# Banded attention and a gated two-layer network on one core: one front moved ahead, units re-dealt to two batches, loads spread anew

## The chip, the core and the metric

The kernel runs on one core of one Trainium2 chip. The metric is the device time of one execution in microseconds, lower is better; the time shown is the median of three runs. The core has five engines that run side by side, each through its own list of instructions in order: PE (TensorE: matmuls and transposes), DVE (VectorE), ACT (ScalarE), POOL (GpSimd) and SP (SyncE, which here only issues DMAs). POOL computes and also issues the loads from memory; an instruction of its list that waits holds up the loads behind it.

## The reference

Attention over a window of 64 keys, for 8 batches of 8 heads, 576 positions and 64 columns a head; then, on the 4608 x 512 result, two matrix products with a gate between them.

```python
scores = scale * np.matmul(q, k.transpose(0, 1, 3, 2))
mask = (rel >= 0) & (rel < window)          # window = 64
attn = softmax(np.where(mask, scores, -1e9))
x = np.matmul(attn, v) ...                  # as 4608 x 512
h = x @ w_in                                # 512 x 2048
g = h * np.clip(h + 3.0, 0.0, 6.0) / 6.0
return g @ w_out                            # 2048 x 512
```

## The kernel before

**Attention** goes by pairs of heads: pair t is heads 2g and 2g+1 of batch b, with b, g = divmod(t, 4); there are 32 pairs. For a pair these steps follow each other:

- `load_qk(b, n, first)` (line 115) issues on POOL the loads of k and then of q for n pairs of batch b, from pair `first` on; 144 KB each for one pair. `load_v(b, part=...)` (131) issues the loads of v in up to three pieces, and `shift(b)` (155) makes on SP a copy of v shifted by 32 partitions.
- `turn(t)` (269): 36 transposes on PE, which put keys and queries of the pair across, into two PSUM banks, tk and tq, of the pool `ps_h`. `turned(t, 0)` copies tk to KT on DVE, `turned(t, 1)` copies tq to QT on ACT (both line 283).
- `s_first(t, host)` and `s_rest(t)` (291, 301): 36 small matmuls, the scores. Those of the first window go into spare columns of the tk and tq banks of another pair, the host; the rest into two banks of `ps_t`.
- `weights(t, ...)` (316): on ACT the exponentials, e0 twice (line 319) and e twice (323); on POOL (batch 1: DVE) three products with the masks, P (328) and Pz twice (331). `front(t, host)` (780) is the scores and the weights together.
- `pv(t)` (383): 40 small matmuls, weights by v, into the pool `ps_o`. `pv_out(t)` (409): six DVE instructions, sums, recs, opg twice, opl twice, which divide by the sums. `x_(t)` (435) turns the result across by DMA transposes on SP into `xT`; for batch 1 `x_turned(t)` (453) does it by five transposes on PE and a copy on ACT.

**The network** goes by blocks of 512 rows, nine in all. A block has 16 first units f0 to f15 (`unit` in `first_units`, 469): four matmuls of 128x512 into one bank, then on ACT t (line 499) and on DVE gT (500); the bank is free when gT is done. It has 16 second units (507), four for each of four groups of 128 rows: four matmuls each over gT into a bank acc; the last of four is followed by a copy osb on ACT (529) and a store. Every unit is thus four matmuls.

**PSUM** has eight banks: `ps_o` two (used as one tile of two), `ps_t` three, `ps_h` two, `ps_acc` one. A tile takes a bank of its pool that was given back; a unit's first matmul waits until the last reader of that bank's former tile is done.

**The order** is written by hand (`manual_schedule`): each engine runs its instructions in the order in which the program gives them. `queue_block(kb, kept, lead)` (540) puts a block's units into a deque, `moe`: first some second units left over from the block before, then the first units with the other left-overs between them, then the block's own second units but for the last `kept`. `weave(n)` takes n units off the front and writes them. `group(t, n)` (752) writes, in this order: pv(t), turn(t+2), the scores and weights of t+1, pv_out(t), the copy KT of t+2, x_(t), two units, the copy QT of t+2, and n - 2 units.

**Around the change** (lines 820 to 868). Batches 0 and 1 have their own order. The loop over t = 4 to 7 does pv of batch 1 and issues loads of batch 2 behind dummy copies (`behind`) that hold POOL back until opg is there. Then come pair 8's turn, the last second units of block 0, the first three quarters of f0 to f3 of block 1 (they lack the last pair, 7), x_turned(7), the last quarters, and group 7, with pair 9's turn, pair 8's scores and four units; behind it on POOL the load of pair 11 and two pieces of v of batch 3. From t = 8 on a group takes 4 units in batch 2 and 8 in each later batch; in the loop the loads of the next batch stand behind the group's products on POOL. While attention runs on, from block 1 on, first units take banks of `ps_t` alone (`late[0] == 1`, line 484).

Of the kernel before, what the change touches and what calls it, by code (L numbers as in the profile page):

```python
# [36 lines left out]
def kernel(  # L37
# [10 lines left out]
    B, H, S, _ = q.shape  # L48
    DM, FF = moe_w_in.shape
    NT = B * S  # L50
    NG = H // 2
# [3 lines left out]
    NFC = FF // P  # L55
# [14 lines left out]
    ps_t = ctx.enter_context(tc.tile_pool(name="ps_t", bufs=3, space=PSUM))  # L70
    ps_h = ctx.enter_context(tc.tile_pool(name="ps_h", bufs=2, space=PSUM))
    ps_acc = ctx.enter_context(tc.tile_pool(name="ps_acc", bufs=1, space=PSUM))
# [42 lines left out]
    def load_qk(b, n=NG, first=0):  # L115
        t = staged[b] if first else stage.tile([P, H, RL * D], BF16, name="qk9", tag="qk")
        hs = slice(2 * first, 2 * (first + n))
        for z, src in enumerate((k, q)):
            nc.gpsimd.dma_start(  # L119
                out=t[halves[z], hs], in_=src[b, hs].rearrange("h (p r) d -> p h (r d)", r=RL)  # L120
            )
        return t
# [8 lines left out]
    def load_v(b, whole=False, part=slice(None)):  # L131
        loads = (
            (0, Un[b % 2][:, 0], 2 * P), (2 * P, Un[b % 2][:, 1], 2 * P),
            *(((W, Us[b % 2][:, 0], 2 * P), (W + 2 * P, Us[b % 2][:, 1], 2 * P)) if whole
              else ((4 * P, Us[b % 2][3 * P // 4 : P, 1], W),)),
        )
        for m, to, n in loads[part]:
            nc.gpsimd.dma_start(  # L138
                out=to[:, :, VO : VO + P],
                in_=v[b, :, m : m + n, :].rearrange("h (p r) d -> p h (r d)", r=2),  # L140
            )
# [13 lines left out]
    def shift(b):  # L155

        un, us = Un[b % 2], Us[b % 2]
        nc.sync.dma_start(out=us[0 : P - 32], in_=un[32:P])
        nc.sync.dma_start(out=us[P - 32 : P, 0], in_=un[0:32, 1])
# [109 lines left out]
    def turn(t):  # L269

        b, g = divmod(t, NG)
        hosts[t] = [ps_h.tile([P, 8 * P], BF16, name=name, tag="bk") for name in ("tk", "tq")]
        for r in range(RL):
            for h in range(2):
                for z in range(2):
                    nc.tensor.transpose(  # L276
                        out=hosts[t][z][halves[h], r * W : (r + 1) * W],
                        in_=staged[b][halves[z], 2 * g + h, r * D : (r + 1) * D],
                        identity=ident[halves[z], halves[z]],
                    )  # L280

    def turned(t, z):
        (nc.scalar.copy if z else nc.vector.tensor_copy)(  # L283
            out=(QT[t % 4][:] if z else KT[t % 4][:, W:]).rearrange("q (p r) -> q p r", r=RL),
            in_=hosts[t][z][:, 0:S].rearrange("q (r p) -> q p r", p=W),
        )
# [177 lines left out]

    gTs = {}
    late = [0]
    halfway, units = {}, {}

    def first_units(kb):
        t0 = kb * TB % XR  # L470
        gT = gpool.tile([P, NFC, TB], BF16, name="gT")
        gTs[kb] = gT

        def unit(fc, gs=range(NG), pool=None, to=None, act=True):
            if fc in halfway:
                hT = halfway.pop(fc)
            elif to is not None:
                hT = to
            else:
                if pool is None:  # L480
                    if late[0] == 0:
                        pool = ps_acc if fc == 8 else ps_h if fc in (5, 6, 11, 12) else ps_t
                    else:
                        pool = ps_t if late[0] == 1 or fc % 2 else ps_h
                hT = pool.tile([P, TB], F32, name="hT", tag="bk")[:]
            for g in gs:
                nc.tensor.matmul(  # L487
                    hT, lhsT=win16[:, g, fc * P : (fc + 1) * P], rhs=xT[:, g, t0 : t0 + TB],
                    start=(g == 0), stop=(g == NG - 1),
                )  # L490
            if gs[-1] == NG - 1 and act:
                hidden(fc, hT)
            else:
                halfway[fc] = hT

        def hidden(fc, hT=None):
            hT = halfway.pop(fc) if hT is None else hT
            t1 = t1pool.tile([P, TB], BF16, name="t1")
            nc.scalar.activation(out=t1[:], in_=hT, func=RELU, bias=half_const[:], scale=1.0 / 6.0)  # L499
            nc.vector.scalar_tensor_tensor(  # L500
                out=gT[:, fc, :], in0=t1[:], scalar=1.0, in1=hT, op0=MIN, op1=MULT
            )

        units[kb] = unit, hidden
        return [lambda fc=fc: unit(fc) for fc in range(NFC)]

    def second_units(kb):
        gT = gTs[kb]
# [27 lines left out]
    moe = deque()  # L536
# [3 lines left out]
    def queue_block(kb, kept=2 * NG, lead=2):  # L540

        f = first_units(kb)
        moe.extend(left[:lead])
        del left[:lead]
        n = len(left)
        for i, unit in enumerate(f):
            moe.extend(left[i * n // NFC : (i + 1) * n // NFC])
            moe.append(unit)
        left[:] = second_units(kb)
        n = len(left) - kept  # L550
        moe.extend(left[:n])
        del left[:n]
# [6 lines left out]
    def pair_bank():  # L559
        both = ps_o.tile([P, 2, 512], F32, name="hTo", tag="o")  # L560
        return [both[:, i] for i in range(2)]

    def complete(kb, fcs, pair=()):
        unit, hidden = units[kb]
        for fc in fcs:
            unit(fc, (NG - 1,), act=fc not in pair)
            if fc in pair[1:]:
                for x in pair:
                    hidden(x)
        for _ in fcs:  # L570
            moe.popleft()

    def weave(n):
        for _ in range(min(n, len(moe))):
            moe.popleft()()
# [94 lines left out]
    staged = {0: load_early_qk((1,))}  # L670
# [64 lines left out]
    u = units[0][0]  # L735
# [16 lines left out]
    def group(t, n):  # L752

        if t >= 2 * NG:
            pv(t)
        if t + 2 < T:
            turn(t + 2)
        if t + 1 < T:
            host = t + 2
            if host >= T:  # L760
                hosts[host] = [ps_h.tile([P, 8 * P], BF16, name=name, tag="bk") for name in ("tk", "tq")]
            s = s_first(t + 1, host)
            weights(t + 1, s, s_rest(t + 1))
        if t >= 2 * NG:
            pv_out(t)
        if t + 2 < T:
            turned(t + 2, 0)
        if t >= 2 * NG:
            x_(t)
        weave(2)  # L770
        if t + 2 < T:
            turned(t + 2, 1)
        weave(n - 2)
# [6 lines left out]
    def front(t, host, muls=(nc.gpsimd,) * 3):  # L780
        s = s_first(t, host)
        weights(t, s, s_rest(t), muls)

    def behind(t):

        nc.gpsimd.tensor_copy(out=seen[:], in_=opgs[t][1][0:1, 0, 0:1])
# [3 lines left out]
    n = NG  # L790
# [29 lines left out]
    for t in range(n, n + 4):  # L820
        pv(t, t % 2 == 0)
        pv_out(t)
        if t < n + 3:
            behind(t)
        if t == n:
            load_v(2, part=slice(1, 3))
        elif t < n + 3:
            load_qk(2, 1, t - n)
        if t > n:
            x_turned(t - 1)  # L830
        if t == n + 2:
            shift(2)
        if t < n + 3:
            weave(1)
    turn_two(2 * NG)
    weave(len(moe))
    late[0] = 1
    queue_block(1)
    u, some = units[1][0], range(NG - 1)
    u(0, some, ps_t)  # L840
    u(1, some, ps_t)
    u(2, some, ps_acc)
    x_turned(n + 3)
    u(3, some, to=pair_bank()[0])
    complete(1, range(4))
    f, z = [moe.popleft() for _ in range(NFC - 4)], list(moe)
    moe.clear()
    moe.extend(f[0:3] + z[0:1] + f[3:6] + z[1:2] + f[6:] + [z[2], z[4], z[3]] + z[5:])
    pads(3, nc.gpsimd.memset)
    group(2 * NG - 1, 4)  # L850
    load_qk(2, 1, 3)
    load_v(3, part=slice(0, 2))
    for t in range(2 * NG, T):
        b, g = divmod(t, NG)
        if g == 0 and b > 2:
            queue_block(b - 1, lead=4 if b == 3 else 2)
        group(t, -(-len(moe) // (NG - g)))
        if b + 1 < B:
            if g == 0:
                staged[b + 1] = load_qk(b + 1, NG if b > 2 else 1)  # L860
            elif b == 2:
                load_qk(b + 1, 1, g)
            if b == 2 and g == 0:
                load_v(b + 1, part=slice(2, 3))
            if b > 2 and g == 1:
                load_v(b + 1)
            if g == 1 + (b > 2):
                shift(b + 1)
    late[0] = 2
    queue_last(NTB - 2)  # L870
# [36 lines left out]
```

## Time and profile before

| | us |
|---|---|
| median of 3 runs | 321.55 (321.15 to 323.0) |
| the profiled execution, in all | 320.98 |
| its span, first to last instruction | 319.3 |
| PE busy | 302.0 |
| ACT busy | 184.3 |
| DVE busy | 181.3 |
| POOL busy | 124.3 |
| mean granted TensorE clock | 0.997 |

The span is shorter than the run by 1.7 us, which lie around it. A busy share is an average: what a stage costs is read from the stage. In the stretch that the change touches, the groups start (first matmul of pv) at 67.99 (pair 8), 72.65 (9), 78.33 (10), 83.81 (11), 88.56 (12), 96.80 (13), 104.97 (14), 113.53 (15) and 121.67 us (16). A line of the trace names the engine, the line of the code, the operation, the tile written and the tiles read; "idle before" and the name behind it say what ended a wait.

### The profile page before, as it was taken

The numbers are of one execution on the slowest core, as the hardware profiler recorded it, in microseconds if no ns is written. First come the engines' busy times: TensorE is split into PE (matmuls) and PEld (weight loads), VectorE is DVE, ScalarE is ACT, GpSimd is POOL, SyncE is SP. The second block draws the span as 40 slices with busy tenths as digits, with TensorE's granted clock in tenths as the row PEclk, the third lists the DMA queues.
The fourth block names the chain that finished last, engine by engine and source line by source line (L and its number), as shares of the span: only waits on it lengthen the run. The fifth ranks groups of instructions, "written<-read, shape, count | busy, mean of one in ns | idle before, by whom it ended". The sixth has DMA issues, their size and how long they took to land.

```text
span 319.3 us, 10688 instructions
## 1 busy us (share of the span) xinstructions
PE 302.0 (95%) x4566; PEld 151.8 (48%) x4608; DVE 181.3 (57%) x415; ACT 184.3 (58%) x345; POOL 124.3 (39%) x168
## 2 busy tenths in 40 slices
PE   7889998998999999999999999999999999999992
PEld 3454454544555455555555555555544444444440
DVE  5766657587737754775377537762776156334200
ACT  2738575586757754776477647764773266454410
POOL 8981206289876335543445345633330000000000
PEclk9999999999999999999999999999999999999998
DMA  6999999939999943994299339934021200100021
GB/s 89 161 210 206 207 192 158 201 51 142 168 140 192 98 118 88 166 130 116 88 158 139 107 100 160 138 105 100 4 69 38 84 33 0 69 33 34 36 75 65
DMA packets 57592, 35.67 MB, mean 112 GB/s; under 512 B 39872, under 2 KB 51648, under 8 KB 57536
## 3 DMA queue, kind: packets, MB, share of 16 engines
q0 software_dynamic: 35904, 18.81, 46.0%
q1 hardware_dynamic: 21632, 16.08, 20.4%
q8 instruction: 38, 0.62, 0.8%
q14 instruction: 18, 0.15, 0.1%
HBM read 37.62 MB, written 9.44 MB: 147 GB/s over the span
## 4 chain that ended last, share of the span: by engine, by line
PE 84%; POOL 5%; DMA 3%; ACT 2%; DVE 2%; issue 2%; POOLq 0%; ACTq 0%; DVEq 0%
PE acc L523 36%; PE hT L487 35%; PE o L404 3%; PE s L310 2%; PE acco L523 2%; PE tk L276 2%; DMA V<-in_v_dram 2%; DMA qk<-in_q_dram 2%; POOL qk L108 2%; POOL Pz L331 1%; PE tq L276 1%; ACT t L499 1%; POOL V L138 1%; POOL qk L119 1%; PE hTo L487 1%
## 5 line engine op out<-in xcount | busy, mean ns | idle before, releaser
L500 DVE SCALAR_TENSOR_TENSOR gT<-t,hT 128x512 bf16<-128x512 bf16 x141 | 95.7, 687 | 78.2 <-ACT t L499 77.2
L487 PE MATMUL hT<-xT,win 128*128 128x512 bf16 x550 | 132.1, 379 | 1.8 <-DVE gT L500 0.6
L523 PE MATMUL acc<-wout,gT 128*128 128x512 bf16 x520 | 126.4, 379 | 2.2 <-issue 1.3
L499 ACT ACTIVATE t<-hT,half_const 128x512 bf16<-128x512 f32 x141 | 95.8, 690 | 48.3 <-PE hT L487 46.5
L487 PEld LDWEIGHTS <-win 128*128 128x128 bf16 x576 | 55.5, 98 | 66.6 <-issue 2.0
L523 PEld LDWEIGHTS <-gT 128*128 128x128 bf16 x576 | 54.5, 98 | 63.2
L331 POOL TENSOR_TENSOR Pz<-e,band 128x512 bf16<-128x512 bf16 x48 | 54.3, 1149 | 0.0
L328 POOL TENSOR_TENSOR P<-e,first 64x256 bf16<-64x256 bf16 x24 | 16.0, 666 | 88.7 <-ACT e L319 88.7
L529 ACT COPY osb<-acc 128x512 f32<-128x512 f32 x34 | 19.9, 586 | 43.1 <-PE acc L523 40.2
L323 ACT ACTIVATE e<-s 128x512 bf16<-128x512 f32 x56 | 30.1, 590 | 0.2 <-issue 0.2
L283 DVE COPY KT<-tk 128x576 bf16<-128x576 bf16 x28 | 21.0, 750 | 5.3 <-ACT e L319 4.5
L138 POOL DMA_DIRECT2D V<-in_v_dram x22 | 17.9, 818 | 8.8 <-DMA wout<-in_moe_w_out_dram 4.6
L428 DVE TENSOR_TENSOR opl<-o,recs 128x256 bf16<-128x256 f32 x52 | 19.7, 420 | 0.5
L283 ACT COPY QT<-tq 128x576 bf16<-128x576 bf16 x28 | 17.8, 637 | 1.5 <-PE tq L276 1.5
L413 DVE TENSOR_REDUCE sums<-o 128x10 f32<-128x20 f32 x26 | 4.6, 176 | 23.6 <-PE o L404 23.6
L404 PEld LDWEIGHTS <-Pz 64*64 64x64 bf16 x1008 | 11.5, 108 | 12.9 <-issue 9.8
L319 ACT ACTIVATE e<-tk 64x128 bf16<-64x128 f32 x28 | 7.6, 271 | 15.1 <-PE tq L296 15.1
L276 PE MATMUL tq<-ident,qk 64*64 64x64 bf16 x504 | 13.9, 195 | 0.6 <-DMA qk<-in_q_dram 0.6
L310 PE MATMUL s<-QT,KT 64*64 64x64 bf16 x896 | 14.1, 195 | 0.4 <-DVE gT L500 0.4
L404 PE MATMUL o<-V,Pz 64*64 64x65 bf16 x936 | 13.6, 195 | 0.8 <-POOL Pz L331 0.8
L276 PE MATMUL tk<-ident,qk 64*64 64x64 bf16 x504 | 14.0, 195 | 0.0
L276 PEld LDWEIGHTS <-qk 64*64 64x64 bf16 x1008 | 11.6, 106 | 2.9 <-issue 2.1
(102 smaller groups left out, 195.9 us busy)
## 6 DMA issues: line engine op xcount, KB each, us to landing
out_dram<-osb SPq DMA_DIRECT2D x36, 256.0 KB, 2.2
V<-in_v_dram POOLq DMA_DIRECT2D x16, 256.0 KB, 5.5
V<-V SPq DMA_DIRECT2D x6, 432.0 KB, 4.3
qk<-in_k_dram POOLq DMA_DIRECT2D x4, 576.0 KB, 7.0
qk<-in_q_dram POOLq DMA_DIRECT2D x4, 576.0 KB, 9.5
wout<-in_moe_w_out_dram POOLq DMA_DIRECT2D x2, 1024.0 KB, 17.3
qk<-in_q_dram POOLq DMA_DIRECT2D x12, 144.0 KB, 4.0
qk<-in_k_dram POOLq DMA_DIRECT2D x12, 144.0 KB, 4.0
```

The lines of the kernel that those rows point to most:

```text
L138: nc.gpsimd.dma_start(out=to[:, :, VO : VO + P], in_=v[b, :, m : m + n, :].rearrange("h (p r) d -> p h (r d)", r=2),)
L276: nc.tensor.transpose(out=hosts[t][z][halves[h], r * W : (r + 1) * W], in_=staged[b][halves[z], 2 * g + h, r * D : (r + 1) * D], identity= ...
L283: (nc.scalar.copy if z else nc.vector.tensor_copy)(out=(QT[t % 4][:] if z else KT[t % 4][:, W:]).rearrange("q (p r) -> q p r", r=RL), in_= ...
L310: nc.tensor.matmul(ss[h][halves[i], c, m, r], lhsT=keys(t, h, W * (w - 1), r), rhs=QT[t % 4][halves[h], w * W : (w + 1) * W], start=True, ...
L323: nc.scalar.activation(out=e[:].rearrange("p c m r w -> p (c m r w)"), in_=ss[h][:].rearrange("p c m r w -> p (c m r w)"), func=EXP, scale ...
L331: muls[h].tensor_tensor(out=Pw[t % 4][:, h].rearrange("p c m r w -> p (c m) (r w)"), in0=e[:].rearrange("p c m r w -> p (c m) (r w)"), in1 ...
L404: nc.tensor.matmul(o[i][halves[c], c0 : c0 + D + 1], lhsT=p, rhs=vt[:, hh, v0 : v0 + D + 1], start=(r == 0), stop=(r == 1), skip_group_che ...
L487: nc.tensor.matmul(hT, lhsT=win16[:, g, fc * P : (fc + 1) * P], rhs=xT[:, g, t0 : t0 + TB], start=(g == 0), stop=(g == NG - 1),)
L499: nc.scalar.activation(out=t1[:], in_=hT, func=RELU, bias=half_const[:], scale=1.0 / 6.0)
L500: nc.vector.scalar_tensor_tensor(out=gT[:, fc, :], in0=t1[:], scalar=1.0, in1=hT, op0=MIN, op1=MULT)
L523: nc.tensor.matmul(acc, lhsT=gT[:, fc, ts * P : (ts + 1) * P], rhs=wout16[:, fc, :], start=(fc == 0), stop=(fc == NFC - 1),)
L529: nc.scalar.copy(out=osb[:], in_=acc)
```

## The change

- **Front of pair 8.** Of block 1 only f0 and f1 have their first three quarters ahead of pair 7's result, f0 in the `ps_o` banks. Then come pair 9's turn and pair 8's scores and weights; then the last quarters of f0 and f1, f2 to f6 whole, and the first second unit. Group 7 is gone as a group; its parts are written out. Eight units of block 1 are written ahead of group 8, as before.
- **Loads.** Pair 10's load leaves the loop over t = 4 to 7. Pairs 10 and 11 are loaded together, 288 KB each for k and q, behind pair 8's products on POOL, followed by one piece of v of batch 3 in place of two. In batch 2, groups 8, 9 and 10 issue the loads of pairs 12, 13, and 14 with 15; v's second piece follows group 8, the third group 9. The shift of batch 3 stays behind group 9. From batch 3 on the loads of the next batch are as before.
- **Units.** Block 1 keeps four second units for later instead of eight. Batch 2 takes five units a group, batch 3 seven, in the order written in `arrange`. There a number from 0 up is a first unit; -1 is the first of the second units in the deque, -2 the second, and so on. Its first units take banks of `ps_h` and `ps_t` in turn, counted from the end of a group, so that the last one has `ps_t`.
- From batch 4 on the units are those of before.

```diff
+        firsts[kb] = [lambda fc=fc: unit(fc) for fc in range(NFC)]
+        return firsts[kb]
@@ loop over t = 4 to 7
-        elif t < n + 3:
-            load_qk(2, 1, t - n)
+        elif t == n + 1:
+            load_qk(2, 1, 1)
@@ after weave(len(moe))
-    queue_block(1)
+    queue_block(1, NG)
     u, some = units[1][0], range(NG - 1)
-    u(0, some, ps_t)
-    u(1, some, ps_t)
-    u(2, some, ps_acc)
+    u(0, some, to=pair_bank()[0])
     x_turned(n + 3)
-    u(3, some, to=pair_bank()[0])
-    complete(1, range(4))
-    f, z = [moe.popleft() for _ in range(NFC - 4)], list(moe)
-    moe.clear()
-    moe.extend(f[0:3] + z[0:1] + f[3:6] + z[1:2] + f[6:] + [z[2], z[4], z[3]] + z[5:])
+    u(1, some, ps_acc)
+    turn(2 * NG + 1)
     pads(3, nc.gpsimd.memset)
-    group(2 * NG - 1, 4)
-    load_qk(2, 1, 3)
-    load_v(3, part=slice(0, 2))
+    front(2 * NG, 2 * NG + 1)
+    load_qk(2, 2, 2)
+    load_v(3, part=slice(0, 1))
+    turned(2 * NG + 1, 0)
+    complete(1, range(2))
+    turned(2 * NG + 1, 1)
+    for fc, pool in zip(range(2, 7), (ps_t, ps_t, ps_h, ps_h, ps_t)):
+        moe.popleft()
+        u(fc, pool=pool)
+
+    def arrange(kb, pools):
+
+        z = {}
+        for i, unit in enumerate(x for x in moe if x not in firsts[kb]):
+            z[i] = unit
+        turn = [ps_h, ps_t]
+        order = []
+        for group_ in pools:
+            fs = [x for x in group_ if x >= 0]
+            for x in group_:
+                if x >= 0:
+                    pool = turn[(len(fs) - fs.index(x)) % 2]
+                    order.append(lambda fc=x, pool=pool: units[kb][0](fc, pool=pool))
+                else:
+                    order.append(z[-1 - x])
+        moe.clear()
+        moe.extend(order)
+
+    moe[NFC - 7]()
+    del moe[NFC - 7]
+    arrange(1, ((7, 8, 9, 10, -1), (11, 12, 13, 14, -2), (15, -4, -5, -3, -6), (-7, -8, -9, -10, -11)))
     for t in range(2 * NG, T):
         b, g = divmod(t, NG)
         if g == 0 and b > 2:
             queue_block(b - 1, lead=4 if b == 3 else 2)
+            if b == 3:
+                arrange(2, (
+                    (-1, -2, 0, 1, 2, 3, -3), (4, 5, -4, 6, 7, 8, -5), (9, -6, 10, 11, 12, 13, -7),
+                    (14, 15, -9, -10, -8, -11, -12),
+                ))
         group(t, -(-len(moe) // (NG - g)))
-        if b + 1 < B:
+        if b == 2:
+            if g < 3:
+                if g == 0:
+                    staged[3] = load_qk(3, 1)
+                else:
+                    load_qk(3, g, g)
+                load_v(3, part=(slice(1, 2), slice(2, 3), slice(0))[g])
+            if g == 1:
+                shift(3)
+        elif b + 1 < B:
...
```

More of the change, by code (lines that the diff above doesn't have):

```diff
@@ L466 @@
     late = [0]
-    halfway, units = {}, {}
+    halfway, units, firsts = {}, {}, {}
     def first_units(kb):
@@ L504, in first_units @@
         units[kb] = unit, hidden
-        return [lambda fc=fc: unit(fc) for fc in range(NFC)]
+        firsts[kb] = [lambda fc=fc: unit(fc) for fc in range(NFC)]
+        return firsts[kb]
     def second_units(kb):
@@ L856 @@
             queue_block(b - 1, lead=4 if b == 3 else 2)
-        group(t, -(-len(moe) // (NG - g)))
-        if b + 1 < B:
-            if g == 0:
[L860 to L865, printed above, removed]
+            if b == 3:
[3 more added lines that the diff above has]
+                ))
+        group(t, -(-len(moe) // (NG - g)))
+        if b == 2:
[8 more added lines that the diff above has]
+        elif b + 1 < B:
+            if g == 0:
+                staged[b + 1] = load_qk(b + 1)
+            if g == 1:
                 load_v(b + 1)
-            if g == 1 + (b > 2):
+            if g == 2:
                 shift(b + 1)
```

## The prediction

> **What bounds the kernel now.** I read the page's parts 1 and 4 first.
>
> ```profile
> PE 302.0 (95%) x4566; PEld 151.8 (48%) x4608; DVE 181.3 (57%) x415; ACT 184.3 (58%) x345; POOL 124.3 (39%) x168
> PE 84%; POOL 5%; DMA 3%; ACT 2%; DVE 2%; issue 2%; POOLq 0%; ACTq 0%; DVEq 0%
> ```
>
> TensorE (PE) sets the end: 95% busy, 84% of the chain of waits. The order of the built programs has the same number of instructions on PE before and after, so nothing is won or lost in work; only PE's waits can change. Next, busy time by stage (columns: window, its length, PE, PEld, DVE, ACT, POOL, granted clock, DMA share, GB/s):
>
> ```profile
> 57.50:68.33 10.83, 9.85 (x159) 4.74 (x157) 6.26 (x12) 8.15 (x16) 4.07 (x8) 1.00 0.56 123
> 68.33:88.56 20.23, 18.55 (x493) 10.05 (x483) 15.40 (x38) 14.04 (x30) 18.36 (x24) 1.00 1.11 145
> 88.56:121.67 33.11, 32.37 (x573) 16.69 (x577) 19.64 (x44) 21.00 (x40) 16.31 (x19) 1.00 0.87 139
> 121.67:154.22 32.55, 32.23 (x581) 16.54 (x588) 19.78 (x44) 20.70 (x40) 15.28 (x17) 1.00 0.70 122
> ```
>
> The rows run from the first turn of batch 2, from pair 10's turn to pv(12) (batch 2), then batches 3 and 4. Batch 4, which the change leaves alone, is four groups with 32 units: a unit is four matmuls, 0.864 us in the chain, so a group costs 32.55/4 - 8 x 0.864 = 1.22 us besides its units. By this price the second window (the rest of a group, 0.87, three more at 1.22, 16 units) would be 18.35 us; it is 20.23, so 1.88 us are waits. Batch 3 has 0.56 us over batch 4. That is all that better cover in batches 2 and 3 can win: 2.44 us. The chain shows where the 1.88 come from:
>
> ```profile
> 71.42 2.21 POOL Pz L331 x2
> 73.63 0.57 POOL qk L119
> 74.20 5.21 DMA qk<-in_q_dram
> 79.41 0.04 issue
> 79.46 0.21 PE tq L276
> ```
>
> POOL is 18.36 of 20.23 us busy there: pv(9) waits for its products, and turn(12) for a load issued behind them.
>
> **What it does, part by part. A: pairs 10 and 11.** Their loads move. Before, pair 10's were issued at 56.27 and 56.85, ahead of front(8), and pair 11's at 67.70. After, one load of both (288 KB each of k and q) stands on POOL's queue behind front(8)'s three products. turn(10), in group 8, waits for it on PE, and behind it stands all else on PE. Working:
> - PE comes to turn(9) at about 60.3: block 0's last unit ends at 58.35; f0's three matmuls now use the bank of pv(7) and wait for opl(7) (58.48); then 0.65, five transposes 0.4, f1's 0.65. Pair 9's q landed at 61.04 (issued 55.26), so turn(9) starts at 61.1, if the traffic then is as before; 60.3 if it lands sooner.
> - From a turn to the end of the last product POOL takes 4.24 us: 88.90 (turn) to 93.14 in the rows below. So 65.3.
> - The load. Page, part 6:
>
> ```profile
> qk<-in_k_dram POOLq DMA_DIRECT2D x4, 576.0 KB, 7.0
> qk<-in_q_dram POOLq DMA_DIRECT2D x4, 576.0 KB, 9.5
> qk<-in_q_dram POOLq DMA_DIRECT2D x12, 144.0 KB, 4.0
> qk<-in_k_dram POOLq DMA_DIRECT2D x12, 144.0 KB, 4.0
> ```
>
>  q is issued 0.65 us after k. So q lands 4.65 us after the products with 144 KB and 10.15 with 576; a third of the way between is 6.5. (The two 288 KB loads of the trace queued behind the weights and are no measure.) turn(10): 65.3 + 6.5 = 71.85, against 68.33 before, with the same eight units of block 1 done ahead of it. **+3.5 us.** Bounds: the quickest small load (3.85 after the products, 83.43 to 87.28) and turn(9) at 60.3 make it 68.4, but f5's product gT, which holds a bank turn(10) needs, then decides, 68.75: +0.4. All of 10.15: +7.1.
>
> [...]
>
> Hidden at the start: POOL's memsets (0.23 each, before e0), scores of pair 8 ahead of f0 and f1 (the same 36 matmuls), the ACT relus queued behind e (they end by 68.7, ahead of turn(10)). Without the load f5's gT would cost the 0.4 above.
>
> **B: five units a group, then seven.** Four units (3.46 us) move from batch 3 to batch 2: nothing in sum. A group of batch 2 is 1.22 + 5 x 0.864 = 5.54 us, POOL's work in it 2.9 us of products and about 2 of issues, so the waits on POOL go. **-1.88 and -0.56.** Bounds: 0 to -2.44. Covered if nothing else is late: pair 12's load (landing near 81, wanted after 86), pairs 14 and 15 (10.5 us after pv(10), wanted at 11.7), block 2's first tile (xT transposed some 8.5 us after pv(11), wanted at 8.7; 0.3 us less cover would cost as much).
>
> **C: units in written order, with banks named.** In the built program f7, f11, f14 and f5, f10, f0 of block 2 use the bank in which that group's keys were just turned (tk), so PE waits for DVE's copy KT; f9 and f13 use the same bank again and wait for gT of f7 and f11. Before, no unit used these two banks in batches 2 and 3. In a group (DVE, ACT and PE of group 12; pv(12) starts at 88.56):
>
> ```profile
> 89.25 0.18 DVE L413 TENSOR_REDUCE sums<-o 128x10 f32<-128x20 f32 x1 [2.42 <-PE o L404]
> 90.19 0.76 DVE L428 TENSOR_TENSOR opl<-o,recs 128x256 bf16<-128x256 f32 x2
> 90.86 0.75 DVE L283 COPY KT<-tk 128x576 bf16<-128x576 bf16 x1
> ...
> 93.26 2.75 PE L487 MATMUL hT<-xT,win 128*128 128x512 bf16 x12
> ...
> 94.32 0.69 ACT L499 ACTIVATE t<-hT,half_const 128x512 bf16<-128x512 f32 x1 [0.28 <-PE hT L487]
> ...
> 95.04 0.69 DVE L500 SCALAR_TENSOR_TENSOR gT<-t,hT 128x512 bf16<-128x512 bf16 x1 [3.43 <-ACT t L499]
> ```
>
> KT ends 3.05 us after pv starts (2.93 to 3.78 in groups 9 to 15), 3.2 where a gT stands before sums. The first unit could start 1.12 after pv (96.80 to 97.93). So a unit at a group's head waits 3.2 + 0.05 - 1.12 = 2.1. From a unit's start to its gT's end is 95.73 - 93.26 = 2.47; a second user of the bank two units (1.73) later waits 0.8, and 0.2 to refill (three matmuls after a pause take 1.04 us, in a stream 0.81): 1.0.
> - Group 8: DVE is ahead, as turn(10) is late; KT only waits for e0 and ends 1.8 after the turn, where f7 could start at 0.78: 1.05, and f9 1.0.
> - Group 9: 2.1 (f11) + 1.0 (f13).
> - Group 13: f5 is second, 2.2 after pv: 1.05 + 0.2.
> - Group 14: f10 third, 3.1: 0.3. Group 12: f0 third: 0. Group 15: f14 at the head: 2.1.
>
> **+8.75 us**; nothing hides it, PE being the engine that waits. Bounds: heads at 1.85 or 2.7 by the KT rows, so 7.3 to 10.7; less than nothing is excluded, the waits being in the program.
>
> **Sum**: 3.5 - 2.44 + 8.75 = +9.8. The profiled execution has a span of 319.3 and 320.98 in all, 0.6 under the median of 321.55; +9.8 on the median is **331.4 us**.
>
> **The rivals.**
> 1. *The load lands early.* A is +0.4, B and C stay: 328.3. For it: small loads land within 4 us on a queue that is idle; against it, the 576 KB rows.
> 2. *The load is slow.* All of 10.15: 335.0. For it: 288 KB rows of 17.5 and 18.6; against: these had 3 MB ahead of them.
> 3. *The clock drops.* Were PE's clock halved after the wait at turn(10), for as long as the wait, 3.4 us, it would cost 1.7 us of work: 333.1. For it: the granted clock is 0.94 in the last 15.3 us, where PE has been idle since 313.1. Against it: 1.00 in every window above; but PE's longest wait there is 0.8 us. [...]
> 4. *The copies come out in time, the other side.* If KT ended before a unit wants its bank, 1.12 us after pv, C would be nothing, and B's 2.44 stands alone once the load is early too: 321.55 + 0.4 - 2.44 = 319.5, faster; with the load late 322.6. The point that decides is the DVE order: KT would have to stand ahead of the six pv_out instructions. For it: in group 8 DVE is free early, and half of f7's wait goes for that reason. Against it: in every other group of the built program KT stands behind them.
>
> **How the numbers follow.** Forecast 0.62, rival 1 0.15, rival 2 0.08, rival 3 0.05, rival 4 0.10 (0.06 faster, 0.04 within). About 0.5% (1.6 us) is what a measurement tells from no change here. Faster 0.06, same 0.04, slower 0.90. The range leaves out rival 4 and the worst of rival 2: from C's low with A's low (321.55 + 0.4 - 2.44 + 7.3 = 326.8) to just over rival 2: 326.5 to 335.5.
>
> **What would show it.** Right: a PE wait of some 3 us for "DMA qk<-in_q_dram" at turn(10), near 68 to 72; PE "hT" waiting for DVE KT by about 2 us in groups 9 and 15 and about 1 us in groups 8 and 13, and for gT by 0.8 in groups 8 and 9; no PE wait for POOL Pz in batch 2; batch 4 as before. Wrong: those KT waits absent or below 0.5 us each, turn(10) without a wait, or a new wait at pv(12) or block 2's first tile.

## The result and the profile after

The changed kernel takes 331.08 us (median of 8 runs, 330.28 to 334.28), the kernel before 322.05 in the same comparison: ratio 1.0281, 95% interval 1.0246 to 1.0317. It is slower by 9.0 us, where 9.8 were forecast. The profiled execution is the longest of the eight, 334.28 us with a span of 332.5; what it lost by a slower clock, below, is more than in the median run. Parts 1 and 4 of its page:

```profile
PE 310.1 (93%) x4608; PEld 153.0 (46%) x4608; DVE 180.8 (54%) x415; ACT 184.1 (55%) x345; POOL 121.8 (37%) x164
PE 82%; DMA 5%; DVE 4%; POOL 3%; ACT 2%; issue 1%; POOLq 0%; ACTq 0%
```

PE still sets the end, but DMA and DVE now hold 9% of the chain, where it was 5%. Busy time by stage, in the columns of the prediction (the third figure from the end, ahead of the DMA share, is the granted clock):

```profile
57.50:69.46 11.96, 11.44 (x235) 5.76 (x234) 7.63 (x18) 8.57 (x17) 5.80 (x11) 1.00 0.71 133
69.46:72.81 3.35, 1.07 (x96) 0.84 (x84) 2.02 (x7) 0.06 (x1) 0.00 (x0) 1.00 1.32 175
72.81:79.64 6.83, 5.99 (x29) 2.21 (x21) 2.13 (x3) 3.71 (x8) 4.98 (x6) 0.50 0.50 76
79.64:100.36 20.72, 18.29 (x405) 9.39 (x403) 11.44 (x28) 11.09 (x24) 11.69 (x14) 1.00 0.77 118
100.36:134.87 34.51, 31.24 (x561) 15.46 (x561) 19.83 (x44) 20.13 (x39) 15.27 (x17) 0.95 0.66 111
...
134.87:167.35 32.48, 32.48 (x577) 16.43 (x576) 19.77 (x44) 20.72 (x40) 15.27 (x17) 1.00 0.72 128
```

Batch 4 (last row) takes 32.48 us, as before. All of the loss lies ahead of it: PE is busy 1.07 of 3.35 us around turn(10); then comes a stretch that looks busy but runs at half the clock; then two batches that wait. The longest waits of PE in that part, from the timeline; the bracket has the length of the wait and what ended it:

```profile
70.71 0.21 PE L276 MATMUL tk<-ident,qk 64*64 64x64 bf16 x1 [1.06 <-DMA qk<-in_k_dram]
72.15 0.21 PE L276 MATMUL tq<-ident,qk 64*64 64x64 bf16 x1 [1.22 <-DMA qk<-in_q_dram]
73.86 6.45 PE L487 MATMUL hT<-xT,win 128*128 128x512 bf16 x16 [0.84 <-DVE KT L283]
84.09 1.89 PE L487 MATMUL hT<-xT,win 128*128 128x512 bf16 x8 [1.79 <-DVE KT L283]
86.61 1.67 PE L487 MATMUL hT<-xT,win 128*128 128x512 bf16 x7 [0.64 <-DVE gT L500]
...
101.52 0.21 PE L276 MATMUL tq<-ident,qk 64*64 64x64 bf16 x1 [0.63 <-DMA qk<-in_q_dram]
...
111.38 0.38 PE L487 MATMUL hT<-xT,win 128*128 128x512 bf16 x1 [0.82 <-DVE KT L283]
...
127.05 3.24 PE L487 MATMUL hT<-xT,win 128*128 128x512 bf16 x8 [1.82 <-DVE KT L283]
```

In this order they are turn(10), twice (for k, then for q), f7, f11, f13, turn(14), f5 and f14: the loads, the units whose bank DVE still had to copy, and f13, whose bank waited for gT of f11. The two rows that last long for their count, 6.45 us for 16 matmuls and 3.24 for 8, are the clock: at full clock a row of 16 takes 3.62 us (the one that starts at 103.99) and a row of 8 takes 1.89 (at 84.09). Group 9 on DVE shows where f11's wait ends:

```profile
81.69 0.18 DVE L413 TENSOR_REDUCE sums<-o 128x10 f32<-128x20 f32 x1
82.62 0.76 DVE L428 TENSOR_TENSOR opl<-o,recs 128x256 bf16<-128x256 f32 x2
83.29 0.75 DVE L283 COPY KT<-tk 128x576 bf16<-128x576 bf16 x1
```

KT ends at 84.04, and f11 starts at 84.09.

From pv(4) to pv(16) the two profiles take 71.79 us (49.88 to 121.67) and 83.38 (51.49 to 134.87), 11.6 more. (The 1.6 us by which pv(4) is late lie in the start, which the change leaves alone; there too this execution ran at half clock, from 11.38 to 14.79.) Term by term, each group's time against the prediction's price, 1.22 us for a group and 0.864 for a unit:

| Term | Forecast, us | Profile, us |
|---|---|---|
| up to the end of group 8's scores | +3.5 | +2.2: waiting for turn(10) sets group 8's scores back by 2.65, the front won 0.46 |
| f7 | +1.05 | +1.0 |
| f9 | +1.0 | 0 |
| group 9 (f11, f13) | +3.1 | +2.64 |
| group 13 (f5) | +1.25 | +0.98 |
| group 14 (f10) | +0.3 | +0.12 |
| group 15 (f14) | +2.1 | +1.87 |
| turn(14) | 0 | +0.77 |
| half clock, groups 8 and 15 | 0 (a rival) | +2.8 and +1.7 |
| waits of the kernel before that are gone | -2.44 | -2.44, if all are |

The profile's terms sum to 11.6. (They count from the start a unit could have had; the idle times in the brackets are shorter, by 0.16 us behind a matmul of 128x512: the trace shows one alone as 0.38 us long, and a row of 8, in 1.89 us, has them 0.216 apart.)

### The profile page after: what moved, and what is told of

Its sections match the earlier page's. It is cut to its first block, busy times and chain, and to the rows that moved or that the text cites. A ratio compares the mean times of both kernels' runs of the same rounds, so it can differ in the third digit from the quotient of the medians.

```text
span 332.5 us, 10729 instructions
## 1 busy us (share of the span) xinstructions
PE 310.1 (93%) x4608; PEld 153.0 (46%) x4608; DVE 180.8 (54%) x415; ACT 184.1 (55%) x345; POOL 121.8 (37%) x164
## 4 chain that ended last, share of the span: by engine, by line
PE 82%; DMA 5%; DVE 4%; POOL 3%; ACT 2%; issue 1%; POOLq 0%; ACTq 0%
PE hT L487 36%; PE acc L524 32%; DMA qk<-in_q_dram 4%; PE o L404 3%; PE acco L524 2%; PE s L310 2%; PE tk L276 2%; DMA qk<-in_k_dram 2%; POOL Pz L331 1%; DVE opl L428 1%; POOL qk L108 1%; PE tq L276 1%; DVE KT L283 1%; ACT t L499 1%; DVE gT L500 1%
## 5 line engine op out<-in xcount | busy, mean ns | idle before, releaser
L487 PE MATMUL hT<-xT,win 128*128 128x512 bf16 x564 | 137.1, 388 | 6.2 <-DVE KT L283 5.3
L524 PE MATMUL acc<-wout,gT 128*128 128x512 bf16 x544 | 129.7, 380 | 0.0
L487 PEld LDWEIGHTS <-win 128*128 128x128 bf16 x576 | 56.4, 99 | 74.8 <-issue 12.0
```

Of the source, the lines that this page charges most:

```text
L487: nc.tensor.matmul(hT, lhsT=win16[:, g, fc * P : (fc + 1) * P], rhs=xT[:, g, t0 : t0 + TB], start=(g == 0), stop=(g == NG - 1),)
L524: nc.tensor.matmul(acc, lhsT=gT[:, fc, ts * P : (ts + 1) * P], rhs=wout16[:, fc, :], start=(fc == 0), stop=(fc == NFC - 1),)
```

## The experiments

**One part undone.** In `e1_load_early` pair 10's load is where it was.

```diff
-        elif t == n + 1:
-            load_qk(2, 1, 1)
+        elif t < n + 3:
+            load_qk(2, 1, t - n)
...
-    load_qk(2, 2, 2)
+    load_qk(2, 1, 3)
```

> The changed kernel with one thing undone: pair 10's load of 144 KB is issued in the loop over t = 4 to 7 again, pair 11's alone behind pair 8's products. Theory (the late load costs): turn(10) no longer waits for a DMA, the 2.6 us in which PE waited at 69.5 to 72.2 shrink to 0.4 at most (f5's gT holds a bank until then), and the halved clock at 72.8 to 79.6 that followed is gone. The time falls by 2.2 (the wait alone) to 5 us (with the clock), to 326 to 329, and the KT waits at f7, f11, f5 and f14 (1.0, 2.0, 1.0 and 2.0 us) stay. Rival (a wait that takes its place): PE stops for gT or for POOL's products in group 8 or 9 instead, and less than 1 us is won, 330 to 331.

Measured: 329.7 us, ratio 1.0236 (1.0199 to 1.0274), above the 326 to 329 that the theory gave. The wait at turn(10) and the half clock behind it are gone from the profile, whose mean clock is 0.995 where the changed kernel's is 0.974, but less was won than the theory said. PE's timeline of groups 8 and 9 has the reason:

```profile
71.14 1.89 PE L487 MATMUL hT<-xT,win 128*128 128x512 bf16 x7 [2.06 <-DVE KT L283]
73.66 1.89 PE L487 MATMUL hT<-xT,win 128*128 128x512 bf16 x8 [0.63 <-DVE gT L500]
79.33 1.89 PE L487 MATMUL hT<-xT,win 128*128 128x512 bf16 x7 [1.79 <-DVE KT L283]
81.85 1.89 PE L487 MATMUL hT<-xT,win 128*128 128x512 bf16 x8 [0.64 <-DVE gT L500]
```

Group 8 now looks like group 9: with turn(10) in time, DVE is no longer ahead, f7 waits 2.06 us in place of 0.84, and f9 its 0.63. The rival was right in part: another wait took the place. The two losses overlap.

In `e2_ps_t` the first units of the groups take `ps_t` alone; loads stay late.

```diff
-                    order.append(lambda fc=x, pool=pool: units[kb][0](fc, pool=pool))
+                    order.append(lambda fc=x: units[kb][0](fc))
```

> The changed kernel with the banks of batches 2 and 3 undone: all first units that are dealt to groups take ps_t, in the same order, five and seven a group; loads as changed. Theory (the banks cost): the four waits for KT and the one for gT at f13 go, 6.9 us in the profile of the changed kernel, and the halved clock behind f14 with them (1.7 us where it comes); some waits for gT on three banks come back, under 1 us. 331.1 falls to 322 to 325; turn(10)'s wait of 2 to 3 us for pair 10 stays. Rival (three banks of which the scores hold two are as tight): the waits move to e and gT, and less than 2 us is won, 329 to 331.

Measured: 324.63 us, ratio 1.0076 (1.0052 to 1.0100). No wait for KT or gT is left on PE in batches 2 and 3: three banks are enough. The wait for pair 10 stays and the clock's drop with it, below.

> Both undone: pair 10's load early and first units on ps_t; the front of pair 8 ahead, five and seven units a group and their order stay. Theory: what is left is the gain of the better cover, 2.4 us at the most, less 0.8 us at turn(14), whose load of two pairs came late: 319.5 to 321.5, at or under the kernel before (ratio 0.993 to 1.0). Rival (the dealing of units or the front itself is slow): over 324, a ratio above 1.006.

Measured (both edits): 320.49 us, ratio 0.9929 (0.9902 to 0.9957). Neither the front nor the dealing is slow. With the ratios of the four kernels the loss comes apart: from this base the banks alone cost 1.0236 - 0.9929 = 3.1%, 9.9 us; the late load alone 1.0076 - 0.9929 = 1.5%, 4.7 us; both together 3.5%, 11.3 us, some 3 us less than their sum. Each ratio is known to about 0.3%, so the 3 us are rough; the waits above show the same overlap.

**Which release f11, f5 and f14 wait for.** In `e4_copy_first` DVE's copy KT is moved ahead of pv_out in groups 8 to 15.

```diff
+        ahead = 2 * NG <= t < 4 * NG
+        if ahead:
+            turned(t + 2, 0)
         if t >= 2 * NG:
             pv_out(t)
-        if t + 2 < T:
+        if t + 2 < T and not ahead:
             turned(t + 2, 0)
```

> The changed kernel, but in groups 8 to 15 the copy KT stands on DVE ahead of the six instructions of pv_out in place of behind them; banks and loads as changed. Theory (PE waits for that copy): KT ends about 1.8 us after the turn, so the waits at f11 and f14 fall from 2.0 to 1.1 us, that at f5 from 1.0 to under 0.2, f7 stays: 2.8 us less, and up to 1.7 more where the clock no longer halves behind f14: 326.5 to 328.5. Rival (PE waits for something else that ends at the same time, e or gT): no change within 0.7 us, 330.4 to 331.8.

Measured: 328.95 us, ratio 1.0190 (1.0145 to 1.0235): 0.9% under the changed kernel, about 2.9 us, a little less than forecast. DVE in group 9, then PE's summed wait:

```profile
82.22 0.76 DVE L283 COPY KT<-tk 128x576 bf16<-128x576 bf16 x1 [0.64 <-ACT e L319]
82.89 0.17 DVE L413 TENSOR_REDUCE sums<-o 128x10 f32<-128x20 f32 x1
```

```profile
PE hT L487 <- DVE KT L283: 2.5, 3, 0.9
```

KT now ends 2.06 us after pv(9) starts in place of 2.93, the changed kernel's waits for it (5.3 us, four of them, the longest 1.8) are 2.5, and none is left at f5. It is this copy that PE waits for.

**The clock.** In `e5_filler` ten matmuls over zeros, which do no work of the kernel, stand in the changed kernel between pv(8) and turn(10).

```diff
+        if t == 2 * NG:
+            warm(ps_t, 10)
         if t + 2 < T:
             turn(t + 2)
```

> The changed kernel with ten matmuls over zeros (128x512, 0.216 us each) into a free ps_t bank between pv(8) and turn(10), where PE otherwise waits 2.7 us for pair 10's load. They do no work of the kernel and end before the load has landed. Theory (the wait also halves PE's clock behind it): the granted clock stays 1.0 in batch 2; turn(10) comes no sooner, but f7 to f10 run at full speed; f9 then waits 0.8 us for gT of f7, which the slow clock hid. 331.1 falls by 1 to 3 us, to 328 to 330, in the executions where the clock had dropped. Rival (the clock's drop is a matter of the execution, not of the wait; or fillers cost as much): no change within 0.7 us, or up to 1 us slower.

Measured: 330.36 us, ratio 1.0241 (1.0205 to 1.0277), a little over the 328 to 330 of the theory; the interval overlaps that of the changed kernel, so the time alone decides nothing. In the profile group 8 runs at full clock (8 matmuls in 1.89 us), and f9 has the wait that the slow clock had hidden:

```profile
73.04 1.89 PE L487 MATMUL hT<-xT,win 128*128 128x512 bf16 x7 [0.88 <-DVE KT L283]
75.56 1.89 PE L487 MATMUL hT<-xT,win 128*128 128x512 bf16 x8 [0.63 <-DVE gT L500]
81.22 0.52 PE L487 MATMUL hT<-xT,win 128*128 128x512 bf16 x1 [1.79 <-DVE KT L283]
81.96 2.34 PE L487 MATMUL hT<-xT,win 128*128 128x512 bf16 x5 [0.22 <-issue]
```

Group 8, pv(8) to pv(9), takes 10.24 us in place of 11.97. But here the matmuls behind f11 run at about half speed, five in 2.34 us, where the changed kernel had eight in 1.89. So the same was tried where no other long wait is near: `e8_ps_t_filler` has the ten matmuls in the kernel of `e2_ps_t`, which ran beside it once more.

> e2_ps_t (first units on ps_t, load of pairs 10 and 11 late) with ten matmuls over zeros between pv(8) and turn(10), which do no work of the kernel and fill most of the 2.8 us that PE waits there. No other long wait is near, so this is the cleaner measure of the clock's share. Theory (the wait also costs the clock): the granted clock stays 1.0 behind turn(10), where e2_ps_t had half for 3.4 us, and the time falls by 1.7 us against e2_ps_t on the same chip: ratio 1.001 to 1.005 against 1.0076. Rival (the clock's drop costs nothing, as f7 to f10 wait for ACT and DVE all the same, or comes anyway): within 0.6 us of e2_ps_t.

> The kernel of e2_ps_t once more, for a comparison with e8_ps_t_filler on one chip: ratio 1.005 to 1.010; in its profile PE's wait at turn(10), 2.5 to 3 us, and a halved clock for one or two stretches of 3.41 us behind it.

Measured: 322.86 us with the filler, ratio 1.0017 (0.9986 to 1.0047), and 324.47 without, 1.0045 (1.0009 to 1.0080). The medians differ by 1.6 us, as the theory had it; the intervals overlap, and the traces decide. Group 8 by window, first of `e2_ps_t`, then with the filler:

```profile
68.06:71.70 3.64, 1.17 (x94) 0.94 (x97) 2.35 (x8) 0.04 (x1) 0.00 (x0) 1.00 1.35 183
71.70:75.12 3.42, 3.20 (x49) 1.43 (x38) 1.10 (x2) 2.16 (x5) 2.78 (x3) 0.50 0.38 61
75.12:78.01 2.89, 2.89 (x14) 1.17 (x12) 1.68 (x4) 2.41 (x4) 2.19 (x4) 1.00 0.55 71
```

```profile
68.42:71.60 3.18, 2.93 (x52) 1.41 (x51) 2.37 (x8) 0.07 (x1) 0.00 (x0) 1.00 1.25 174
71.60:76.83 5.23, 5.14 (x91) 2.56 (x91) 2.77 (x5) 4.39 (x9) 4.06 (x5) 1.00 0.44 59
```

The group takes 9.95 us without the filler (10.35 in `e9_ps_t_again`) and 8.41 with it. Without it the half clock fills 3.42 us of the group. So the clock's drop costs about 1.5 us here; the load lands no sooner with the filler (q 3.2 us after pv(8) starts in both).

**Towards a faster version.** `e6_single_loads` is `e3_both` with pairs 14 and 15 loaded one by one.

```diff
-            if g < 3:
-                if g == 0:
-                    staged[3] = load_qk(3, 1)
-                else:
-                    load_qk(3, g, g)
-                load_v(3, part=(slice(1, 2), slice(2, 3), slice(0))[g])
+            if g == 0:
+                staged[3] = load_qk(3, 1)
+            else:
+                load_qk(3, 1, g)
+            if g < 2:
+                load_v(3, part=(slice(1, 2), slice(2, 3))[g])
```

> Pair 10's load early and first units on ps_t as in e3_both; besides, pairs 14 and 15 are loaded singly, behind groups 10 and 11, in place of together behind group 10. Theory: e3_both's last wait of batch 3, 0.75 us at turn(14) for k of two pairs, goes: ratio 0.990 to 0.992, 319.1 to 319.9. Rival: it goes on to turn(15), whose load now starts a group later: as e3_both, 0.993.

Measured: 319.3 us, ratio 0.9892 (0.9865 to 0.9919), the fastest of all, and 1.1% under the kernel before, with an interval that leaves out 1. The gain over `e3_both` is as forecast, but within the intervals; the profile has no wait at turn(14). Its batches 2, 3 and 4:

```profile
68.34:90.83 22.49, 22.15 (x526) 11.87 (x529) 15.67 (x39) 14.42 (x32) 17.71 (x22) 1.00 0.95 134
90.83:119.88 29.05, 28.84 (x557) 14.92 (x560) 19.84 (x44) 20.01 (x39) 15.42 (x18) 1.00 0.96 141
119.88:152.36 32.48, 32.16 (x573) 16.43 (x576) 19.77 (x44) 20.72 (x40) 15.28 (x17) 1.00 0.75 129
```

Batch 2 is four groups and 20 units, by the prices of the prediction 22.2 us, batch 3 four and 28, 29.1: they run at the steady pace, 0.3 us off it, where the kernel before lost 2.4.

In `e7_old_front` the front alone goes back, in that kernel.

```diff
-    u(0, some, to=pair_bank()[0])
+    u(0, some, ps_t)
+    u(1, some, ps_t)
+    u(2, some, ps_acc)
     x_turned(n + 3)
-    u(1, some, ps_acc)
-    turn(2 * NG + 1)
+    u(3, some, to=pair_bank()[0])
+    complete(1, range(4))
+    f, z = [moe.popleft() for _ in range(NFC - 4)], list(moe)
+    moe.clear()
+    moe.extend(f[0:3] + z[0:1] + f[3:] + z[1:])
...
-    front(2 * NG, 2 * NG + 1)
+    group(2 * NG - 1, 4)
```

> As e6_single_loads, but with the front as it was before the change: three quarters of f0 to f3, then group 7, pair 8's scores behind them. The five and seven units a group, their order and the loads stay. It tells the front from the dealing. Theory (the gain is the dealing's cover over POOL and the loads, 1.9 us in batch 2 and 0.4 in batch 3): within 0.8 us of e6_single_loads, ratio 0.991 to 0.995. Rival (the front ahead is the gain: PE's small waits at 61 to 66 us of the kernel before, 1.5 us in sum, and POOL's products 2 us sooner): ratio 0.997 or more.

Measured: 320.1 us, ratio 0.9930 (0.9891 to 0.9968), 0.8 us over `e6_single_loads` by the medians. From pv(8) to pv(16) it takes 51.59 us, `e6_single_loads` 51.54 and the kernel before 53.68: the 2.1 us won there are the dealing's and the loads'. The front can only show ahead of pv(8). From pv(4) to pv(8) the kernel before takes 18.11 us and the nine profiles with the new front 17.13 to 17.89, so it seems to win 0.2 to 1.0 us; `e7_old_front` itself is no measure of it there (18.95, with a wait of 1.4 us inside pv(4)). The intervals of the timed ratios overlap, so they can't tell this gain from nothing.

## Why the prediction was right, and where not

The forecast was 331.4 us, the median is 331.08. The direction and the two mechanisms were right, and the experiments show both. That the sum came so near is in part luck: two terms were too large, and two costs were missing. Two sums of the prediction are off by little: C's terms add up to 8.8, not 8.75, and a load that lands 4 us behind 65.3, as rival 1 has it of small loads, makes A +1.0; the +0.4 of that rival needs turn(9) at the early bound or the load in 3.4 us.

- **A, the late load.** Mechanism right, +3.5 forecast, +2.2 in the profile. turn(9) did not wait for pair 9 (q landed at 61.64, PE came at 62.07), and the load of two pairs landed 5.6 us after pair 8's last product (66.46 to 72.10), not 6.5: interpolating between 144 and 576 KB was 0.9 us too careful.
- **B, more units in batch 2.** Right in kind. `e3_both` and `e6_single_loads` show that the waits on POOL and on pair 12 go and that nothing else takes their place; the prediction called 2.44 us all there is to win, and from pv(4) to pv(16) `e6_single_loads` takes 69.44 us against 71.79, 2.35 less, 0.2 of it ahead of pv(8). Its timed ratio, 0.9892, is 3.5 us under the kernel before (interval 2.6 to 4.4), a little more than that; where the rest comes from isn't shown.
- **B's covers.** One failed. Pairs 14 and 15 were to be there 10.5 us after pv(10); q landed 12.2 after it (89.29 to 101.48), its own landing 7.2 us long, and turn(14) waited 0.77. The other covers held.
- **C, the banks.** Mechanism right in every place named but f9's; +8.75 forecast, 6.6 in the profile. The units at the head of a group cost 1.9, not 2.1; in group 9 KT ended 2.93 us after pv, the low end of the prediction's rows. The 0.2 us to refill, which f9, f13 and f5 were charged, did not show: f13 starts 0.8 us late in all, and its matmuls follow each other in steps of 0.215 us at once. The prediction read it from three matmuls that take 1.04 us (at 97.93); the first two of them start 0.44 us apart, two steps, as if one between them were missing from the trace. f9's 1.0 did not appear because f8 ran at half clock while f7's gT was made; with the filler it is there, 0.8 us. The prediction saw that DVE is ahead in group 8 and priced f7 at 1.05 (1.0 measured); it did not say that A and C therefore can't be undone one without the other, which `e1_load_early` showed.
- **The rivals.** 1 and 2 did not come. 3, the clock, did, beside the forecast, and at waits shorter than it assumed (1.06 and 1.22 us at turn(10), 1.82 at f14): 4.5 us in the profiled execution, the longest of eight. Its 3.4 us at half clock were the author's estimate, and no run shows a stretch as long as the wait: behind turn(10) the clock was 0.50 for 6.83 us in the changed kernel and for 3.42 in `e2_ps_t`. In the median run it is less. The mean clock on record is 0.974 in the two longest runs, 0.986 in the next two and 0.990 in the four shortest. Over 329 us, 0.990 is 6.6 us at half clock; in the profiled execution 3.7 of its 17.3 us at half clock lie at the very end, and if that is so in the others, about one stretch of 3.4 us is left, an estimate of some 1.7 us of lost work. The other terms and the ratio leave about 2. 4 did not come: KT stands behind pv_out in all groups, and moving it (`e4_copy_first`) wins about 0.9%, not the whole of C.

## What to carry to other kernels

When units of work are dealt to PSUM banks by hand, look, for each unit, at the last reader of the bank's former tile and at what stands ahead of that reader on its engine: an idle bank is only free once that engine's queue has come to it (here KT ended 2.93 us after pv(9) started, behind pv_out, and 2.06 ahead of it). Move a load only with the queue it is moved behind in mind; here one load put behind three products cost more (4.7 us by the ratios) than all the cover that the rest of the change won (2.4). And undo parts in pairs as well as singly, since two waits at one place hide each other (here the late load and the banks cost 11.3 us together, some 3 less than singly).

## What the runs showed of the hardware

PE's granted clock was 0.50 behind waits shorter than the 3.4 us that the prediction took. Two stretches of the changed kernel around f14, in the columns above:

```profile
124.01:127.43 3.42, 1.60 (x115) 1.37 (x115) 2.89 (x8) 1.40 (x4) 1.80 (x3) 1.00 0.26 87
127.43:130.84 3.41, 3.41 (x9) 1.22 (x8) 0.69 (x1) 1.20 (x2) 1.07 (x1) 0.50 0.23 43
```

Here it was a wait of 1.82 us (125.23 to 127.05), in a stretch with 1.60 us of PE work, most of it small matmuls, and the clock was 0.50 for 3.41 us behind it. At turn(10) two waits, of 1.06 and 1.22 us, were followed by 0.50 for 6.83 us (72.81 to 79.64).

The length of a wait does not tell whether the clock drops. In the same execution f11 waits 1.79 us (82.30 to 84.09), and the clock stayed: the eight matmuls behind it take 1.89 us. With the filler f11 again waits 1.79 us, and five matmuls behind it take 2.34. Two more waits of this length left the clock as it was. One is f14's in `e5_filler`, 1.82 us:

```profile
122.28:125.70 3.42, 1.55 (x99) 1.23 (x86) 2.53 (x8) 1.40 (x4) 2.17 (x3) 1.00 0.15 40
125.70:129.11 3.41, 3.41 (x18) 1.52 (x16) 1.37 (x2) 1.90 (x3) 0.71 (x1) 1.00 0.17 33
```

The stretch of that wait has 1.55 us of PE work, about as much as the 1.60 above. The other is f11's in `e1_load_early`, 1.79 us, with eight matmuls in 1.89 us soon behind it (at 81.85). What decides was not shown.

The start shows a drop too, in a part that no edit touches: the profile of the changed kernel has 3.41 us at half clock from 11.38 to 14.79, where that of the kernel before is at 1.00. And one kernel gets different clocks from run to run: the mean clock of the six executions of `e7_old_front` is between 0.978 and 0.998. So compare two profiles by the stage, and look at the clock first.
